# Sharing the 64-row remainder of two products in one step of the array

## The chip, the cores and the metric

The kernel runs on one core of a Trainium2 chip. The metric is the device time of one execution in microseconds (us); the kernel before took 552.86 us, the median of three runs (552.03 to 553.38). The change counts as seen where it moves this time by more than the runs differ.

## The reference

The input `x` has 2048 rows of 448 features. The output is `g * a + (1 - g) * b`, with a gate `g` per row, an attention with a compressive memory (`a`) and a feed-forward network (`b`). Cut to what matters:

```python
q, k, v = x @ wq, x @ wk, x @ wv       # 448 -> 448 = 16 heads of 28
for s in range(4):                     # segments of 512 rows
    p = softmax(qs @ ks.T * scale + mask)
    a_mem = (phi(qs) @ M) / (phi(qs) @ z + 1e-6)
    o = sigmoid(beta) * a_mem + (1 - sigmoid(beta)) * (p @ vs)
    M, z = M + phi(ks).T @ vs, z + phi(ks).sum()
a = o @ wo                             # 448 -> 448
b = silu(x @ w1) @ w2                  # 448 -> 1792 -> 448
g = sigmoid((x * gate_w).sum(-1))
```

Everything is float32. Five products have the 448 features as the dimension that is summed over: q, k, v (with the gate's weights as an extra column), the first half of the feed-forward network, and the output projection `o @ wo`.

## The kernel before

**Products.** Each float32 operand is scaled by a power of two and split into two float16 halves, a high one and a low one (what the rounding left over). A product is then the sum of high x high, low x high and high x low. The 448 features are three chunks of 128 rows and a remainder of 64. For a chunk of 128 the three terms are three matmuls. The remainder is stored twice, in partitions 0 to 63 and again in 64 to 127. Of `x` the remainder's slot has the high half above and the low half below (`x16`, L526), and the weights' two slots have their high half twice and their low half twice. So two matmuls of 128 rows do the remainder: the one with the weights' high half gives high x high and high x low, the other gives low x high (and low x low). A product is 3 x 3 + 2 = 11 matmuls (`passes`, L369; `product`, L532, whose matmuls all have L540).

**Which products there are.** `proj` (L798) makes q and k of one group of four heads and one segment: 128 output rows, 512 columns, 16 products each, in the `mm` banks of PSUM. The 16 rows of a group that q and k leave free carry the last 128 columns of the network's first weights. `vproj` (L852) makes v of 128 rows of `x`: 450 columns, 16 products, in the `sc` banks. `unit` (L1051) makes a block of 128 of the network's 1792 inner features for one segment, 512 columns, in the `mm` banks; after these products it adds up the second half of the network (L1086). `last_part` (L1280) projects the attention's output of 128 rows with `wo`, 448 columns, in the `sc` banks. `halves` (L513) makes the high and low halves of an operand: one instruction on ScalarE for the high half, one on VectorE, or two on GpSimd, for the low half. `features` (L554) does so for the attention's output and has it transposed by a DMA.

**Stages.** `project` loads `x` and the weights, finds their largest values (`scales`, L399, which spreads a value over all partitions with a matmul of one or two rows at L427), makes q, k, v and the memory, and stores them in DRAM. The second stage runs the attention of 16 groups and, between its matmuls, the first pass of the feed-forward network: 10 of the 14 blocks, in four segments. Then the second pass takes the three blocks left (and the one that came with q and k) and adds everything up.

**Order.** A planner (`Sched`) writes the instructions of each engine in a fixed order. It simulates the five queues from costs in the code: a task becomes ready when what it depends on has ended, and of the ready tasks the one with the lowest priority number goes first. A product is four tasks: one for each chunk of three matmuls, one for the remainder's two. Rings of buffers (`Ring`, `Buf`) hold a task back until a buffer is free; PSUM has three `mm`, three `sc` and two `cc` banks at first (L38) and four, three and one later (L39). The numbers at the head of the file (VF, VS, OT1 and so on) shift priorities; they change nothing in what is computed.

Of the kernel before, what the change touches and what calls it, by code (L numbers as in the profile page):

```python
# [46 lines left out]
WOT = -23.27  # L47
# [9 lines left out]
LOP = 33.77  # L57
LATE = 0.08
FIRST = 104.18
WPRIO = 134.65  # L60
MAXO = 62.72
# [3 lines left out]
MP = 34.45  # L65
# [11 lines left out]
XH0 = -8.84  # L77
XLD = -11.75
# [6 lines left out]
PRICE = 25.59  # L85
PVRUNS = [((1, 0), 1)]
PVP = 81.22
FLO = -69.24
FHI = 869.75
WOP = 155.66  # L90
SZ = 30.78
# [3 lines left out]
XLEAD = 146.82  # L95


class Ring:
    def __init__(self, n, make, shared=True):
        self.n, self.make, self.seq, self.shared = n, make, [], shared  # L100
# [7 lines left out]
class Task:  # L108
    def __init__(self, eng, dur, fn, deps, takes, uses, prio, lat, port):
        self.costs = {eng: dur} if isinstance(eng, str) else dict(zip(eng, dur))  # L110
        self.eng, self.fn, self.prio, self.lat, self.port = None, fn, prio, lat, port
        self.deps, self.takes, self.bufs = deps, takes, set(takes) | set(uses)
        self.banks = [b for b in self.bufs if not b.ring.shared]
        self.end, self.nd, self.succ = None, 0, []
        self.lead, self.tail = 0.0, 1.0


class Sched:
# [36 lines left out]
    def start_of(self, t, eng):  # L155
        s = max(self.ready(t, eng), self.free[eng])
        for b in t.takes:
            q = b.ring.seq
            k = len(q) - b.ring.n
# [34 lines left out]
    def run(self, until=None):  # L194
        wait = set(until) if until is not None else None
        while wait is None or wait:
# [29 lines left out]
            for b in t.takes:  # L226
                b.ring.seq.append(b)
                b.v = b.ring.make()
# [18 lines left out]
def infini_mix(ctx: ExitStack, tc: tile.TileContext, x, wq, wk, wv, wo, beta, w1, w2, out):  # L247
# [119 lines left out]
    X16 = {s: base.tile([128, 7, L], F16, name=f"xh{s}") for s in range(NSEG)}  # L367
# [158 lines left out]
    def x16(s, c, prio):  # L526
        ALL, END = slice(None), slice(REM, 128)
        r, d = XR.pop((s, c))
        lo = [((ALL, 4 + c), (ALL,), (ALL, c)) if c < NC else ((END, NC), (END,), (END, NC))]
        XH[s, c] = halves(NSEG - 1 - s, (ALL, c), lo, lambda: X16[s], lambda: r.v, L, d, prio, uses=[r])  # L530

    def product(ps, pairs, cols, prio, deps=(), takes=(), uses=(), cuts=None, kind=None):  # L532
        kind = kind or ful
        cuts = cuts or [3] * (NC) + [2]
        last, i0, n = None, 0, sum(cuts)
        for c, m in enumerate(cuts):
            def go(i0=i0, m=m):
                p = pairs()
                for i in range(i0, i0 + m):
                    nc.tensor.matmul(ps(), *p[i], start=(i == 0), stop=(i == n - 1))  # L540
            d = deps[c] if isinstance(deps, dict) else deps
            last = pe(kind(cols, m), go, last, *d, takes=takes if c == 0 else (), uses=tuple(takes) + tuple(uses), prio=prio)
            i0 += m
        return last

# [8 lines left out]
    def features(ol, half2, ot, ready, prio):  # L554

        sc, edge = os[:, 1:2], NC * 128
        hi = copy(D + 110, lambda: nc.scalar.activation(half2.v[:, :D], ol.v, AF.Copy, scale=sc), *ready, takes=[half2],
                  uses=[ol], prio=prio)

        def lo(e):  # L560
            rest(e, half2.v[:, D:L], ol.v[:, edge:], sc, half2.v[:, edge:D])
# [12 lines left out]
    def get_wa(f, ring, prio, *deps, got=None):  # L574
        (r, d), w = got or fetch_wa(f, prio, *deps), Buf(ring)

        def v():
            return r.v.rearrange("p (a b) -> p a b", a=4)
        WA[f] = (w, halves(W1, (slice(None), slice(0, 4)), [((slice(None), slice(4, 8)), (slice(None),), (slice(None), slice(0, 4)))],
                           lambda: w.v, v, L, d, prio, takes=[w], uses=[r]))  # L580
        return WA[f][1]
# [93 lines left out]
    def project():  # L675
# [88 lines left out]
        def whalves(name, prio, places):  # L764
            ALL = slice(None)
            for c, (b, _, v) in enumerate(places):
                k = dict(prio=prio + 0.01 * c)
                if name == "v":
                    def dst():
                        return W["v"][:, :, :D]  # L770
                    WS[name][c] = halves(WV, (ALL, c), [((ALL, 4 + c), (ALL,), (ALL, c))], dst, lambda v=v: v()[:, :D], D,
                                         SCALED[WV], uses=[b], **k)
                    continue
# [4 lines left out]
                for j, sl, n in ((WQ if name == "q" else WK, slice(0, GW), D), (HQ if name == "q" else HK, slice(GW, 128), 64)):  # L778
                    def src(v=v, sl=sl):
                        return v().rearrange("p (g e) -> p g e", g=NG)[:, :, sl]  # L780
                    WS[name][c] += halves(j, (ALL, c, ALL, sl), [((ALL, 4 + c, ALL, sl), (ALL,), (ALL, c, ALL, sl))], dst, src, n,
                                          SCALED[j], uses=[b], **k)
# [13 lines left out]
        PQ, PK, VB, MH, RT = {}, {}, {}, {}, {}  # L796

        def proj(t, which, prio):  # L798
            s, g = divmod(t, NG)
            w = W[which][:, :, g * 128:(g + 1) * 128]  # L800
            ps, hl = Buf(BK["mm"]), Buf(R["stg"])
            need = (s > 0) if which == "q" else (s < NSEG - 1)
            p = product(lambda: ps.v, lambda: passes(w, X16[s]), L, prio,
                        deps={c: WS[which][c] + XH[s, c] for c in range(NC + 1)}, takes=[ps], kind=half)
# [47 lines left out]
        def vproj(k, prio):  # L852
            s, tb = divmod(k, TB)
            ps, v = Buf(BK["sc"]), Buf(VT)
            p = product(lambda: ps.v[:, :D + 2],
                        lambda: passes(W["v"], X16[s][:, :, tb * 128:(tb + 1) * 128], True), D, prio,
                        deps={c: WS["v"][c] + WS["g"] + XH[s, c] for c in range(NC + 1)}, takes=[ps], kind=half)
# [120 lines left out]
        for t in range(NT):  # L978
# [5 lines left out]
            proj(t, "q", o)  # L984
            proj(t, "k", o + 1)
            if g == 0:
                for k in range(TB):
                    vproj(s * TB + k, VP(o, k))
# [55 lines left out]
    WAR2 = tiles(fp, "wa2", [128, 8, 128], F16, len(PASSES[0]) - NA)  # L1044
# [6 lines left out]
    def unit(s, fs, prio, finish, gate=(), tail=False):  # L1051
        gt = {}
        t1, t2 = {}, {}
        for f in fs:
            if f == FREE:
                gt[f] = spare(s, prio(0), m)
                continue
            p0 = prio(11 * L)
            ps, th, g = Buf(BK["mm"]), Buf(TH), Buf(GTR)
            w, wd = WA[f]  # L1060
            m = product(lambda ps=ps: ps.v, lambda w=w: passes(w.v, X16[s]), L, p0, deps=wd + PREV,
                        takes=[ps, g], uses=[w], kind=half)
# [10 lines left out]
            PREV[:] = [m]  # L1073
# [206 lines left out]
    def last_part(s, tb, ps, lasts, prio):  # L1280
        k = s * TB + tb
        ol, pl, oh, ot, pw, a, y = Buf(OL), Buf(PL), Buf(OH), Buf(OT), Buf(BK["sc"]), Buf(AR), Buf(YR)
        pr = prio - WOP
        rows = slice(tb * 128, (tb + 1) * 128)
        more = (Buf(ML), attended, amscr[s][:, tb]) if s else None
        d1 = load_o(ol, oscr[s][rows, :], *OST[s], PRE.get("o"), more=more, prio=pr - WOP)
        d2 = dma(229e3, lambda: start(pl.v, pscr[s][rows, :]), PST[k], *attended, PRE.get("p"),
                 takes=[pl], prio=pr - WOP)
        PRE.update(o=d1, p=d2)
        ft = features(ol, oh, ot, [d1, outer, PRE.get("f")], pr - WOT)  # L1290
        m = product(lambda: pw.v[:, :D], lambda: passes(wos.v, ot.v, True), D, pr,
                    deps={c: ft + WOS[c] for c in range(NC + 1)}, takes=[pw], uses=[ot], kind=half)
# [78 lines left out]
```

## Time and profile before

| what | before |
|---|---|
| median of three runs | 552.86 us (552.03 to 553.38) |
| profiled execution | 551.7 us from the first to the last instruction; the profile gives no other time of it |
| TensorE matmuls | 4009, busy 534.8 us (97%) |
| VectorE, ScalarE, GpSimd | busy 409.3, 391.8 and 354.7 us |
| mean granted TensorE clock | 0.984 of full speed |

PE is TensorE and PEld its weight loads, DVE is VectorE, ACT ScalarE, POOL GpSimd and SP SyncE, which issues the DMAs. A matmul's own duration reaches to its modelled end, and neighbours overlap; what a matmul costs in a dense stream is the distance from its start to the next one's. A row of the order of time gives the start in us, the length in us, the engine, the line, the operation, what is written from what, the array's rows and columns in use, the moving operand, and how many like it follow each other.

### The profile page before, as it was taken

What the parts mean: (1) busy time and instruction counts of PE and PEld (TensorE: products, weight loads), DVE (VectorE), ACT (ScalarE), POOL (GpSimd) and SP (SyncE); (2) the same over time, 40 slices, a digit from 0 to 9 for tenths busy, and PEclk for the clock granted to TensorE, in tenths of its full rate; (3) what the DMA queues carried; (4) which work ended last, traced back from release to release, by engine and by line L of the source; (5) the groups of instructions that cost most, each with busy time, mean ns of one, the idle gap of its engine ahead of it and who ended that gap; (6) DMA issues with size and microseconds to landing.
All of it is one profiled execution on the core that took longest, in us unless ns stands there. A gap on an engine that the chain in (4) does not pass through costs nothing.

```text
span 551.7 us, 11563 instructions
## 1 busy us (share of the span) xinstructions
PE 534.8 (97%) x4009; PEld 294.7 (53%) x4009; DVE 409.3 (74%) x1074; ACT 391.8 (71%) x688; POOL 354.7 (64%) x519
## 2 busy tenths in 40 slices
PE   4699999999999999999999999999999999999997
PEld 1234655655554556555665555655555555555444
DVE  6889999899789966777666779766987319646473
ACT  1588898986656977899877997878998896402140
POOL 2063254845830689988999987999999995213120
PEclk8689999999999999999999999999999999999999
DMA  8658998885586434312433234434301515698962
GB/s 276 205 175 227 203 236 233 225 226 166 170 233 162 146 100 137 87 42 80 121 102 102 58 98 124 121 103 112 100 18 53 138 49 152 219 241 212 225 160 83
DMA packets 89194, 81.68 MB, mean 148 GB/s; under 512 B 55176, under 2 KB 78856, under 8 KB 89136
## 3 DMA queue, kind: packets, MB, share of 16 engines
q1 hardware_dynamic: 89136, 80.95, 53.1%
q8 instruction: 31, 0.51, 0.4%
q14 instruction: 27, 0.22, 0.1%
HBM read 48.41 MB, written 26.09 MB: 135 GB/s over the span
## 4 chain that ended last, share of the span: by engine, by line
PE 89%; DVE 4%; DMA 4%; ACT 1%; issue 1%; SPq 0%; DVEq 0%; ACTq 0%
PE mm L540 31%; PE mm L1086 23%; PE sc L540 12%; PE sc L1182 6%; PE sc L644 6%; PE cc L1216 6%; DMA rawf<-in_w_dram 2%; PE cc L932 1%; DMA xraw<-in_x_dram 1%; PE cc L895 1%; DVE sizes L388 1%; DVE sc L654 1%; DMA v_scr<-vt 1%; PE sc L640 1%; PE cc L933 0%
## 5 line engine op out<-in xcount | busy, mean ns | idle before, releaser
L1203 POOL TENSOR_TENSOR phl<-pf,phl 128x384 f16<-128x384 f32 (+1 forms) x192 | 189.5, 1008 | 16.2 <-ACT phl L1199 16.2
L1086 PE MATMUL mm<-wb,ghl 128*128 128x448 f16 (+1 forms) x684 | 148.8, 349 | 0.0
L540 PE MATMUL mm<-xh,wa 128*128 128x512 f16 x572 | 141.4, 379 | 0.0
L1187 ACT ACTIVATE pf<-sc,es 128x512 f32<-128x512 f32 (+1 forms) x192 | 109.7, 623 | 19.8 <-PE sc L1182 18.6
L654 DVE CUSTOM_DVE_ANT_0 sc<-sc,mk 128x384 f32<-128x384 f32 (+1 forms) x192 | 104.8, 572 | 20.4 <-PE sc L644 19.1
L1086 PEld LDWEIGHTS <-ghl 128*128 128x128 f16 x684 | 65.0, 97 | 52.5 <-DVE ghl L508 0.3
L1199 ACT ACTIVATE phl<-pf 128x1280 f16<-128x1280 f32 x64 | 81.3, 1277 | 14.9 <-POOL pf L1193 14.9
L540 PEld LDWEIGHTS <-wa 128*128 128x128 f16 x572 | 53.6, 97 | 54.4 <-issue 1.4
L1182 PE MATMUL sc<-ring 86*128 86x512 f16 (+3 forms) x256 | 59.3, 299 | 0.4 <-ACT pf L1187 0.2
L644 PE MATMUL sc<-ring 84*128 84x128 f16 (+3 forms) x256 | 58.2, 299 | 0.1
L1224 DVE TENSOR_REDUCE oraw<-cc 128x116 f32<-128x232 f32 x64 | 25.3, 395 | 30.8 <-PE cc L1216 30.6
L1063 ACT ACTIVATE th<-mm,ths 128x512 f32<-128x512 f32 x52 | 35.8, 699 | 16.0 <-PE mm L540 15.8
L1216 PEld LDWEIGHTS <-phl 128*128 128x128 f16 x1280 | 41.9, 96 | 9.1
L540 PE MATMUL mm<-xh,wqs 128*128 128x512 f16 x176 | 44.5, 390 | 1.0 <-ACT wqs L516 0.7
L551 POOL TENSOR_TENSOR ol<-ol,ml 128x448 f32<-128x448 f32 x12 | 13.7, 1138 | 48.7 <-DMA ol<-o_scr 37.2
L1065 DVE SCALAR_TENSOR_TENSOR mm<-th,mm 128x512 f32<-128x512 f32 x52 | 35.7, 694 | 10.9 <-ACT th L1063 10.9
L1216 PE MATMUL cc<-vg,phl 128*128 128x29 f16 (+1 forms) x1280 | 43.6, 182 | 0.0
L540 PE MATMUL sc<-wvs,xh 128*128 128x450 f16 x176 | 39.9, 368 | 3.1 <-ACT wvs L516 2.1
L540 PE MATMUL mm<-xh,wks 128*128 128x512 f16 x176 | 42.1, 380 | 0.0
L1069 DVE SCALAR_TENSOR_TENSOR ghl<-mm,ghl 128x512 f16<-128x512 f32 x52 | 35.1, 683 | 5.6 <-ACT ghl L1067 5.2
L1182 PEld LDWEIGHTS <-ring 86*128 86x128 f16 x256 | 23.8, 97 | 22.0 <-issue 1.1
L1067 ACT ACTIVATE ghl<-mm 128x512 f16<-128x512 f32 x52 | 30.9, 604 | 6.5 <-DVE mm L1065 6.4
(165 smaller groups left out, 835.9 us busy)
## 6 DMA issues: line engine op xcount, KB each, us to landing
rawf<-in_w_dram SPq DMA_DIRECT2D x26, 256.0 KB
rawf<-in_w_dram SPq DMA_DIRECT2D x28, 224.0 KB
xraw<-in_x_dram SPq DMA_DIRECT2D x16, 256.0 KB
v_scr<-vt SPq DMA_DIRECT2D x16, 232.0 KB
vg<-v_scr SPq DMA_DIRECT2D x16, 232.0 KB
q_scr<-stg SPq DMA_DIRECT2D x16, 224.0 KB
ring<-q_scr SPq DMA_DIRECT2D x16, 224.0 KB
k_scr<-stg SPq DMA_DIRECT2D x16, 224.0 KB
```

What stands on the lines that cost most here:

```text
L540: nc.tensor.matmul(ps(), *p[i], start=(i == 0), stop=(i == n - 1))
L644: nc.tensor.matmul(ps.v[:, u:u + n], rg.v[:KS, 0, hh, i * 128:(i + 1) * 128], rg.v[:KS, 1, hh, :n], start=(i > 0), stop=(i > 0 or j == 3), ...
L654: nc.vector.tensor_tensor_reduce(r, r, MK[:, L - n:], 1.0, NEG, OP.add, OP.max, mx.v[:, hh, i:i + 1])
L1063: e1 = sact(L, lambda ps=ps, th=th: nc.scalar.activation(th.v, ps.v, AF.Tanh, scale=ths[:, s:s + 1]), m, DER[s], takes=[th], uses=[ps], pr ...
L1065: e2 = dve(L, lambda ps=ps, th=th: nc.vector.scalar_tensor_tensor(ps.v, th.v, 1.0, ps.v, op0=OP.add, op1=OP.mult), e1, uses=[ps, th], prio=p0)
L1069: e4 = dve(L, lambda ps=ps, g=g: nc.vector.scalar_tensor_tensor(g.v[:, 1], ps.v, DOWN, g.v[:, 0], op0=OP.mult, op1=OP.subtract), e3, uses= ...
L1086: nc.tensor.matmul(ps.v[:, lo:hi], g.v[:, y, sl], w.v[:, z, lo:hi], start=(j == 0 and i == 0), stop=(j == len(fs) - 1 and i == 2))
L1182: nc.tensor.matmul(ps.v[:, e:e + w], rg.v[:KK, 1, hh, j * 128:(j + 1) * 128], rg.v[:KK, 0, hh, j * 128:], start=True, stop=True)
L1187: ex.append(sact(e, lambda b=b, ps=ps, pf=pf, e=e: nc.scalar.activation(pf.v[:, b, :e], ps.v[:, :e], AF.Exp, scale=es[:, s:s + 1]), m, *ex ...
L1199: hi = copy(1280, lambda hl=hl, flat=flat: nc.scalar.activation(hl.v[:, 0], flat(), AF.Copy), *mk, takes=[hl], uses=[pf], prio=p0 + 2)
L1203: low = pool(w - u, lambda hl=hl, flat=flat, u=u, w=w: nc.gpsimd.tensor_sub(hl.v[:, 1, u:w], flat()[:, u:w], hl.v[:, 0, u:w]), low, uses=[ ...
L1216: nc.tensor.matmul(p[:, i, :2 - z], hl.v[:, z, u:u + 128], vg.v[:, j, hh, :2 - z], start=(z == zs[0] and i == 0), stop=(z == zs[-1] and j ...
```

## The change

The remainder's terms are dealt out anew. The weights' slot now has the high half in one half of its rows and the low half in the other, and `x` has its high half in both halves of one slot and its low half in both halves of another. One matmul of 128 rows gives high x high and low x high; high x low is left for a matmul of 64 rows. Low x low falls away. Two products (a and b) form a pair: a's ten full matmuls, then one joint step with a's 64-row matmul in partitions 0 to 63 and b's in 64 to 127, each into its own PSUM bank, then b's ten full matmuls. Pairs are two groups of q, two of k, two row blocks of v, two blocks of the network, and two row blocks of the output projection. With three blocks in the second pass one block per segment has no partner; its 64-row matmul stands alone (`product2` with `b` as `None`).

The planner counts the joint step as one matmul. A pair of one kind begins after the joint step of the pair before it, and while a pair is open, its ring keeps a bank for b. The weights' preparation follows the new layout: the low half of the last chunk is made for 64 rows only, in some places as an instruction of its own; v gets one copy (`same`), and every other block of the output projection gets a second instruction on ScalarE. `x` takes eight slots for seven, and one tile for weights seven for eight. The priority numbers are drawn anew, and the memory reserved for another kind of DMA descriptors is set to 4096 bytes.

```diff
-WOT = -23.27
+SCRATCH = 4096
+QB = 2.0
+KA = 1.93
+KB = 4.0
+WOT = 40.43
...
-FIRST = 104.18
-WPRIO = 134.65
-MAXO = 62.72
+FIRST = 96.7
+WPRIO = 137.54
+MAXO = 75.89
...
-VF = 0.02
-VA = 1.68
-VS = 15.54
+VF = 0.61
+VA = 0.01
+VS = 20.73
 NV = 8
-XS0 = 16.16
-VC = -4.07
-OT1 = -16.51
-XS = 17.15
-QS = -15.23
+XS0 = 13.14
+VC = -72.55
+OT1 = 4.96
+XS = 15.92
+QS = -18.08
...
-WOP = 155.66
+WOP = 27.88
...
+            if b.ring.open is not None and b is not t.closes and k >= b.ring.open - 1:
+                return None
...
-    def passes(w, a, flip=False):
+    X16 = {s: base.tile([128, 8, L], F16, name=f"xh{s}") for s in range(NSEG)}
+
+    HALF = (slice(0, REM), slice(REM, 128))
+
+    def passes(w, a, last=(NC, NC)):
+
         r = []
         for c in range(NC):
             r.append((w[:, c], a[:, c]))
             r.append((w[:, 4 + c], a[:, c]))
             r.append((w[:, c], a[:, 4 + c]))
-        r.append((w[:, NC], a[:, NC]))
-        r.append((w[:, 4 + NC], a[:, NC]))
-        return [(z, y) for y, z in r] if flip else r
+        r.append((w[:, last[0]], a[:, last[1]]))
+        return r
...
+    def chunks(x, before, first, pair=False):
+
+        last = None
+        for c, m in enumerate([3] * NC + [1]):
+            def go(c=c, m=m):
+                p = x.pairs()
+                for i in range(3 * c, 3 * c + m):
+                    nc.tensor.matmul(x.view(), *p[i], start=(first and i == 0), stop=(not first and i == 3 * NC),
+                                     skip_group_check=True)
+            last = pe(half(x.cols, m), go, last, *(before if c == 0 else ()), *x.deps[c],
+                      takes=x.takes if first and c == 0 else (), uses=x.uses, prio=x.prio)
+            if pair and c == 0:
+                last.opens = x.takes[0]
         return last
+
+    def product2(a, b=None, before=()):
+
+        last = chunks(a, before, True, b is not None)
+
+        def go():
+            z, y = a.rest(0)
+            nc.tensor.matmul(a.view(), z, y, start=False, stop=True, skip_group_check=True)
+            if b:
+                z, y = b.rest(1)
+                nc.tensor.matmul(b.view(), z, y, start=True, stop=False, skip_group_check=True)
+        joint = pe(half(a.cols), go, last, *(b.deps[NC] if b else ()), takes=b.takes if b else (),
+                   uses=a.uses + (b.uses if b else []), prio=a.prio)
+        joint.closes = b and b.takes[0]
+        return joint, (chunks(b, (joint,), False) if b else None)
...
+            rest(e, half2.v[:, el], ol.v[:, edge:], sc, half2.v[:, eh])
...
+        ALL, E = slice(None), HALF[1 - f % 2]
+        lo = [((ALL, slice(4, 4 + NC)), (ALL, slice(0, NC)), (ALL, slice(0, NC))), ((E, NC), (E, NC), (E, NC))]
...
+                def same(e):
+                    e.tensor_copy(W["v"][HALF[0], 4 + NC], W["v"][HALF[0], NC])
+                WS["v"][NC] = WS["v"][NC] + [either(D // 2, same, *WS["v"][NC], *WS["g"], prio=prio + 0.1)]
...
+            if g % 2 == 0:
+                proj(t, "q", (o, o + QB))
+                proj(t, "k", (o + KA, o + KB))
```

More of the change, by code (lines that the diff above doesn't have):

```diff
@@ L226, in run @@
             for b in t.takes:
+                if b is t.opens or b is t.closes:
+                    b.ring.open = len(b.ring.seq) if b is t.opens else None
                 b.ring.seq.append(b)
@@ L526, in x16 @@
     def x16(s, c, prio):
-        ALL, END = slice(None), slice(REM, 128)
+        ALL = slice(None)
         r, d = XR.pop((s, c))
[L529 to L543, printed above, removed]
-        return last
+        XH[s, c] = halves(NSEG - 1 - s, (ALL, c), [((ALL, 4 + c), (ALL,), (ALL, c))], lambda: X16[s], lambda: r.v, L, d, prio,
+                          uses=[r])
@@ L1053, in unit @@
         t1, t2 = {}, {}
[L1054 to L1062, printed above, removed]
+        blocks = [f for f in fs if f != FREE]
+        ends = {}
+        for f in blocks[::2]:
+            two, gs = [], [Buf(GTR) for _ in blocks[f - blocks[0]:][:2]]
+            for i, g in enumerate(gs, f):
+                p0, ps = prio(11 * L), Buf(BK["mm"])
+                w, wd = WA[i]
+                gt[i] = g
+                two.append(Prod(ps, lambda ps=ps: ps.v, lambda w=w: passes(w.v, X16[s]),
+                                lambda h, w=w: (w.v[HALF[h], NC], X16[s][HALF[h], 4 + NC]), L, p0, wd, takes=[] if two else gs, uses=[g, w]))
+            done = product2(*two, before=PREV)
+            PREV[:] = done[:1]
+            for x, end in zip(two, done):
+                ends[f + two.index(x)] = x.takes[0], x.prio, end
+        for f in blocks:
+            ps, p0, m = ends[f]
+            th, g = Buf(TH), gt[f]
             e1 = sact(L, lambda ps=ps, th=th: nc.scalar.activation(th.v, ps.v, AF.Tanh, scale=ths[:, s:s + 1]), m, DER[s], takes=[th],
```

144 lines of the change are left out of this document (96 added, 48 removed).

## The prediction

> **What bounds the kernel now.** I read the page first, then busy time by stage, then the matmuls by form, then the order of single matmuls where the array changes its use. On the page:
>
> ```profile
> span 551.7 us, 11563 instructions
> PE 534.8 (97%) x4009; PEld 294.7 (53%) x4009; DVE 409.3 (74%) x1074; ACT 391.8 (71%) x688; POOL 354.7 (64%) x519
> ...
> PE 89%; DVE 4%; DMA 4%; ACT 1%; issue 1%; SPq 0%; DVEq 0%; ACTq 0%
> ```
>
> TensorE is busy 97% of the span and carries 89% of the chain that ended last. The sum is made against this execution, whose only time is its span of 551.7 us; the median of the runs, 552.86 us, stands 1.2 us above it, and I add the change to the median. By stage (columns: stretch and its length, busy us of each engine with its instructions, granted clock, DMA share, GB/s):
>
> ```profile
> 0.00:33.00 33.00, 20.26 (x68) 7.69 (x69) 25.66 (x77) 14.18 (x33) 8.09 (x33) 0.74 0.70 237
> 33.00:190.00 157.00, 156.84 (x880) 85.30 (x879) 142.78 (x356) 123.61 (x258) 77.00 (x124) 1.00 0.76 203
> 190.00:440.00 250.00, 249.71 (x2393) 145.14 (x2392) 180.19 (x537) 210.90 (x329) 231.77 (x322) 1.00 0.34 93
> 440.00:551.70 111.70, 108.02 (x672) 56.53 (x670) 60.68 (x107) 43.10 (x69) 37.80 (x43) 1.00 0.61 168
> ```
>
> ```profile
> 548.06 0.81 DVE L1297 SCALAR_TENSOR_TENSOR y<-mm,ogs,ya 128x224 f32<-128x224 f32 x2 [0.47 <-PE mm L1086]
> ```
>
> From 33 us on TensorE misses 0.16, 0.29 and 3.68 us, the last nearly all behind its last matmul, which this DVE row at 548.06 waits for and the output's transfer follows. What it gains there the kernel gains, and what it loses the kernel loses. The other engines have room: the nearest, POOL, has 18 us left in the third stage. Only the first 33 us wait for others. But busy time overlaps between neighbours, so the price of a matmul has to be read from starts (start us, length, then the group and its count):
>
> ```profile
> 519.71 1.68 PE L540 MATMUL sc<-wos,oT 128*128 128x448 f16 x8
> 521.22 2.97 PE L540 MATMUL mm<-xh,wa 128*128 128x512 f16 x13
> ```
>
> Eight matmuls of 448 columns take the 1.51 us to the next start, 0.189 each. Thirteen of 512 take 2.97 with the last one's full length of 0.38, so (2.97 - 0.38)/12 = 0.216 each.
>
> **What is removed.** The products over the 448 features:
>
> ```profile
> L540 PE MATMUL mm<-xh,wa 128*128 128x512 f16 x572 | 141.4, 379 | 0.0
> L540 PE MATMUL mm<-xh,wqs 128*128 128x512 f16 x176 | 44.5, 390 | 1.0 <-ACT wqs L516 0.7 <-DVE wqs L508 0.3
> L540 PE MATMUL mm<-xh,wks 128*128 128x512 f16 x176 | 42.1, 380 | 0.0
> L540 PE MATMUL sc<-wvs,xh 128*128 128x450 f16 x176 | 39.9, 368 | 3.1 <-ACT wvs L516 2.1 <-DVE wvs L508 0.9
> L540 PE MATMUL sc<-wos,oT 128*128 128x448 f16 x176 | 35.4, 353 | 0.0
> ```
>
> A product is 11 matmuls, so these are 52 FFN products (13 blocks, 4 segments) and 16 each for q, k, v and o. A pair goes from 22 full matmuls to 20 and one joint step. The FFN gives 5 pairs per segment in the first pass (10 blocks), and one pair and one single in the second (3 blocks): 24 pairs and 4 singles. With 8 pairs each for q, k, v and o there are 40 pairs of 512 columns and 16 of 448 or 450. Were a joint step as cheap as one full matmul, 40 x 0.216 + 16 x 0.189 = 11.7 us would go.
>
> **What a joint step costs.** No step of 64 rows is in the trace. Its neighbours lie on both sides. Above are steps of 86 rows, below the steps of one or two rows in the scaling (L427):
>
> ```profile
> 127.86 1.46 PE L540 MATMUL mm<-xh,wqs 128*128 128x512 f16 x6
> 129.25 0.17 PE L427 MATMUL cc<-diag,oneb 2*128 2x2 bf16 x1
> 129.35 1.25 PE L540 MATMUL mm<-xh,wqs 128*128 128x512 f16 x5
> 130.44 0.81 PE L540 MATMUL mm<-xh,wks 128*128 128x512 f16 x3
> ```
>
> ```profile
> 342.81 0.73 PE L1086 MATMUL mm<-wb,ghl 128*128 128x448 f16 x3
> 343.47 0.17 PE L427 MATMUL cc<-diag,oneb 1*128 1x1 bf16 x1
> 343.57 0.74 PE L1086 MATMUL mm<-wb,ghl 128*128 128x448 f16 x3
> 344.15 0.27 PE L1182 MATMUL sc<-ring 86*128 86x256 f16 x1
> 344.26 0.73 PE L1086 MATMUL mm<-wb,ghl 128*128 128x448 f16 x3
> ```
>
> From 127.86 to 130.44 lie 11 full matmuls and one L427: 2.58 - 11 x 0.216 = 0.206 us for L427, which streams two columns. In the second place 1.34 - 6 x 0.189 = 0.206 us again. The 86-row step behind it takes 0.11 us for 256 columns, with nothing added. The weight loads tell why (start, length):
>
> ```profile
> 343.46 0.09 PEld L427 LDWEIGHTS <-oneb 1*128 1x128 bf16 x1 [0.37 <-issue]
> 343.57 0.10 PEld L1086 LDWEIGHTS <-ghl 128*128 128x128 f16 x1
> ...
> 343.57 0.11 PEld L1086 LDWEIGHTS <-ghl 128*128 128x128 f16 x2
> ```
>
> L427's load has nothing to wait for, yet it starts at 343.46, 0.08 us after the last full matmul has streamed (342.81 + 3 x 0.189 = 343.38), and the next full load waits until 0.10 us after L427's matmul. So the array empties before and after, where full loads otherwise run under the matmul ahead. I take 0.206 us as the price of going into row tiles and out again. The bounds are that of 86 rows (nothing) and this one; I take this one, since 86 rows cannot share the array in halves and a step that uses a part of the rows as a tile is what both L427 and the joint step are. Of the two 64-row matmuls the second can follow by the distance of two loads that do not wait for each other: the last row has two loads of 0.10 us in 0.11, so 0.015 us. The bounds for that are 0 and a whole load, 0.10.
>
> "Changing tiling mode (not just tile) drains the TensorE" is how the Trainium skill has it in TensorEngine Tiling (Array Packing), Key Properties. By that rule the 64-row step pays like L427 and the sum is the one below; by the 86-row rows it would be 541.5 us, which is the first rival. The skill's TensorE: Matmul & The Clock Gate, Part 3, gives about 4 ns between tiles; no run here shows it, and with it the sum would be 0.6 us lower.
>
> A joint step of 512 columns then costs 0.206 + 0.216 + 0.015 = 0.437 us where two full matmuls took 0.432; one of 448, 0.410 against 0.378. A single keeps 11 steps, the last of them a 64-row one: 0.206 more. Sum: 40 x 0.005 + 16 x 0.032 + 4 x 0.206 = 0.20 + 0.51 + 0.82 = **+1.5 us**. The gain of 11.7 us is paid back in changes of the array's use.
>
> **What is added beside it.** Nearest rows:
>
> ```profile
> L508 DVE SCALAR_TENSOR_TENSOR wa<-rawf,up,wa 128x512 f16<-128x512 f32 x12 | 10.9, 917 | 1.9 <-ACT wa L516 1.9
> L508 DVE SCALAR_TENSOR_TENSOR oh<-ol,os,oh 128x64 f16<-128x64 f32 x15 | 4.5, 303 | 4.9 <-ACT oh L557 4.9
> L557 ACT ACTIVATE oh<-ol,os 128x448 f16<-128x448 f32 x16 | 10.7, 669 | 34.3 <-POOL ol L551 34.3
> ```
>
> The low half of each FFN weight block becomes two instructions: 13 x 0.30 = 4 us on DVE or POOL, as do those of the q and k weights' last chunk (at most 4 x 0.3). Eight odd blocks of o get a second ACT instruction, at most 8 x 0.67 = 5.4 us. DVE is idle for 70 us of the third stage and ACT for 69 of the last, so these cost nothing; uncovered, each delays its product by its own length. One copy of the v weights (448 columns, at most the 0.92 us of a wa block) stands ahead of the first v product's last chunk; nine earlier matmuls of 0.19 or more cover it. No DMA is added or moved to another queue, and evictions keep their number. A pair takes its second bank at the joint step, some 0.2 us before b's first full matmul; what waits behind a missing bank is all of TensorE, but with four mm banks in the FFN (L39) and no wait of the FFN products in the groups above, I cost it at nothing.
>
> **The redrawn order** can only count in the head, and it is there that the rows show room:
>
> ```profile
> 23.93 2.26 PE L540 MATMUL sc<-wvs,xh 128*128 128x450 f16 x11
> ...
> 27.21 0.27 PE L418 MATMUL cc<-ident,most 128*2 128x128 f32 x1 [0.43 <-DVE most L414]
> 28.21 0.39 PE L540 MATMUL mm<-xh,wqs 128*128 128x512 f16 x1 [0.73 <-ACT wqs L516]
> 28.89 2.21 PE L540 MATMUL mm<-xh,wqs 128*128 128x512 f16 x5 [0.29 <-DVE wqs L508]
> 31.03 0.18 PE L427 MATMUL cc<-diag,oneb 2*128 2x2 bf16 x1
> 31.15 1.45 PE L540 MATMUL mm<-xh,wqs 128*128 128x512 f16 x3
> 32.40 1.34 PE L540 MATMUL sc<-wvs,xh 128*128 128x450 f16 x6
> ```
>
> TensorE idles 0.43 + 0.73 + 0.29 = 1.45 us, and after that matmuls of 512 columns come every 0.43 us (28.89 to 31.03, five), twice their price, for nine of them until 32.40: 9 x 0.21 = 1.9 us. A v product more as filler would save up to 3.4 us; one less (11 x 0.19) would cost 2.1. The scale of v's gate is moved up (VC), which frees v's banks earlier, the others of segment 0 move back (OT1); I take -0.5 us. Forecast: 552.86 + 1.5 - 0.5 = **553.9 us**, no measurable change.
>
> **The rivals.** *The array does not empty for 64-row tiles.* For it: steps of 86 rows cost nothing extra. Against: L427. Then -11.7 + 56 x 0.015 - 0.5 = -11.4, 541.5 us; were only one of the two passages free, 60 x 0.103 = 6.2 less than forecast, 547.7. *The second tile's load waits.* The second matmul starts a whole load after the first, 0.10 for 0.015, at 56 places: +4.8, 558.7 us, slower. It is decisive from 0.03 us of distance on (553.9 + 56 x 0.015 = 554.7). For it: L427's load too started only when it was alone. Against: the two overlapping loads at 343.57. *The tiles run one after the other*, which would mean that the change does not do what it says: 40 x 0.201 + 16 x 0.174 = 10.8 more, 564.7. Nothing in the trace excludes it. *The head is filled*: all 3.4 us gone, 2.9 below the forecast, 551.0; the v matmuls that already stand in it speak for it, v's three banks against.
>
> **How the numbers follow.** Chances: forecast 0.48 (its own range 552 to 556), no emptying 0.14, one passage free 0.08, head filled 0.08, load waits 0.16, one after the other 0.06. About 0.3%, 1.7 us, is what a measurement of this kernel can tell: the bounds are 551.2 and 554.5. Faster: 0.14 + 0.08 + 0.05 of the filled head + 0.03 of the forecast = 0.30. Slower: 0.16 + 0.06 + 0.14 of the forecast = 0.36. The rest, 0.34, is no change. The range leaves out no emptying and one after the other (0.20) and reaches past one free passage and the waiting load, with an us or less of the head on either side: 547 to 559.5.
>
> **What would show it.** In the trace after: x520 where x572 stood, 160 in place of each 176, and 64-row matmuls at the joint line, 116 in all; their first load some 0.1 us after the stream before it has ended, the two starts some 0.015 us apart, the next full load 0.1 us after the stream's end, and 0.44 us from joint step to next start. Loads that run under the matmul ahead would show the first rival, starts 0.1 apart the second, 0.2 apart the third. TensorE should stay without idle time from 33 us on; stalls for a bank would make the forecast wrong in a way that I have not priced.

## The result and the profile after

| | before | after |
|---|---|---|
| median of four runs each | 552.57 us (552.03 to 553.38) | 557.75 us (557.30 to 559.27) |
| ratio, 95% interval | | 1.0095 [1.0077, 1.0113] |
| profiled execution, span | 551.7 us | 557.6 us (the other three: 555.6 to 556.4) |

The change makes the kernel slower by 0.95%, 5.2 us by the medians and 5.9 us between the two profiled executions, each of them the longest of its four. The forecast was 553.9 us, counted from 552.86 us, the median of three of the four runs before. First the page of the kernel after:

```profile
PE 535.5 (96%) x4009; PEld 284.6 (51%) x4009; DVE 416.0 (75%) x1090; ACT 394.2 (71%) x696; POOL 349.6 (63%) x519
...
PE 81%; DVE 10%; POOL 2%; DMA 2%; ACT 2%; issue 1%; SPq 0%; DVEq 0%; POOLq 0%
```

TensorE is busy 0.7 us longer with the same number of matmuls, and VectorE's part of the chain that ended last has gone from 4% to 10%. Hardly any work became longer; waits came. Where, the stages tell. The kernel after, by stretch (length, busy us of PE, PEld, DVE, ACT and POOL with their instructions, granted clock, DMA share, GB/s):

```profile
0.00:33.00 33.00, 21.36 (x80) 8.01 (x80) 26.37 (x81) 13.73 (x32) 8.04 (x35) 0.79 0.68 220
33.00:140.00 107.00, 105.81 (x608) 55.55 (x606) 96.51 (x252) 88.97 (x198) 55.39 (x92) 1.00 0.81 213
140.00:160.00 20.00, 18.00 (x103) 9.58 (x103) 18.82 (x47) 10.45 (x22) 10.57 (x17) 1.00 0.66 195
...
180.00:200.00 20.00, 17.64 (x130) 9.08 (x129) 19.85 (x56) 13.96 (x22) 10.43 (x14) 1.00 0.48 137
200.00:440.00 240.00, 238.93 (x2269) 136.34 (x2267) 175.20 (x515) 203.19 (x320) 216.80 (x305) 1.00 0.34 94
440.00:557.60 117.60, 113.75 (x732) 57.08 (x730) 62.64 (x108) 48.16 (x81) 42.62 (x50) 1.00 0.57 161
```

The kernel before, in those of the same stretches that the prediction does not show:

```profile
33.00:140.00 107.00, 107.00 (x612) 59.27 (x611) 101.07 (x267) 88.56 (x195) 55.52 (x90) 1.00 0.81 210
140.00:160.00 20.00, 20.00 (x114) 11.45 (x113) 15.48 (x32) 11.45 (x22) 14.58 (x24) 1.00 0.65 194
...
180.00:200.00 20.00, 19.94 (x165) 11.29 (x164) 16.95 (x46) 17.46 (x29) 13.82 (x18) 1.00 0.50 144
200.00:440.00 240.00, 239.71 (x2286) 139.06 (x2284) 172.13 (x513) 203.22 (x317) 224.03 (x313) 1.00 0.34 92
```

Length less busy time is what TensorE idles:

| us | before | after | difference |
|---|---|---|---|
| 0 to 33 | 12.74 | 11.64 | -1.1 |
| 33 to 140 | 0.00 | 1.19 | +1.2 |
| 140 to 160 | 0.00 | 2.00 | +2.0 |
| 180 to 200 | 0.06 | 2.36 | +2.3 |
| 200 to 440 | 0.29 | 1.07 | +0.8 |
| 440 to the end | 3.68 | 3.85 | +0.2 |

With 0.10 us less in the stretch left out, the idle time grows by 5.2 us; with the 0.7 of busy time that is the 5.9 us. Nearly all of it is waits from 33 to 440 us, where before there were almost none. They repeat: a second profile of the same kernel (taken beside the late pairs below) idles 1.19, 2.00, 2.21 and 1.17 us from 33 to 140, 140 to 160, 180 to 200 and 200 to 440. In both stretches that lose 2 us VectorE has become nearly full: 18.82 of 20 us for 15.48, and 19.85 for 16.95. That alone makes no wait: from 33 to 140 us it was busy 101.07 of 107 us before, and TensorE idled 0.00.

The joint step itself, in the order of time (start us, length, group, count):

```profile
44.13 0.39 PE L572 MATMUL mm<-xh,wqs 64*128 64x512 f16 x1
44.13 0.39 PE L575 MATMUL mm<-xh,wqs 64*128 64x512 f16 x1
...
159.26 4.49 PE L558 MATMUL mm<-xh,wa 128*128 128x512 f16 x20
163.68 0.39 PE L572 MATMUL mm<-xh,wa 64*128 64x512 f16 x1
163.68 0.39 PE L575 MATMUL mm<-xh,wa 64*128 64x512 f16 x1
164.00 4.49 PE L558 MATMUL mm<-xh,wa 128*128 128x512 f16 x20
```

and the weight loads of the first one:

```profile
44.13 0.09 PEld L572 LDWEIGHTS <-wqs 64*128 64x128 f16 x1 [0.42 <-issue]
44.13 0.09 PEld L575 LDWEIGHTS <-wqs 64*128 64x128 f16 x1
44.45 0.55 PEld L558 LDWEIGHTS <-wqs 128*128 128x128 f16 x4 [0.23 <-issue]
```

The two 64-row matmuls start in the same hundredth, and so do their loads: the tiles do run at once. So it is at 54 of the 56 joint steps; at the other two the second starts 0.05 and 0.13 us later. But the twenty full ones have streamed at 159.26 + 20 x 0.216 = 163.58 and the step starts at 163.68, 0.10 later; and the next full load (44.45) waits until 0.10 after the step has streamed (44.13 + 0.216 = 44.35). The array empties on both sides. Steps of 448 columns do the same (16 x 0.189 us after 483.70 is 486.72):

```profile
483.70 3.19 PE L558 MATMUL sc<-wos,oT 128*128 128x448 f16 x16
486.82 0.36 PE L572 MATMUL sc<-wos,oT 64*128 64x448 f16 x1
...
487.12 2.07 PE L558 MATMUL sc<-wos,oT 128*128 128x448 f16 x10
```

A pair of 512 columns repeats after 164.00 - 159.26 = 4.74 us, and 22 full matmuls took 22 x 0.216 = 4.75.

Then the waits. All 1.19 us between 33 and 140 stand at 36 to 39 us, where k's products wait for the halves of k's weights. The last of them, on TensorE and on VectorE:

```profile
39.08 0.38 PE L558 MATMUL mm<-xh,wks 128*128 128x512 f16 x1 [0.42 <-DVE wks L519]
```

```profile
38.48 0.93 DVE L519 SCALAR_TENSOR_TENSOR wks<-wa,up,wks 64x224 f16<-64x224 f32 x2
```

These two instructions of 64 rows stand where the kernel before has one of 128 rows; they take 0.93 us, one of 128x448 at 34 us takes 0.67. The longest wait is at 154 us. TensorE, and what GpSimd does meanwhile:

```profile
152.68 1.51 PE L558 MATMUL sc<-wvs,xh 128*128 128x450 f16 x7
155.72 0.38 PE L1006 MATMUL cc<-mhl,phq 112*128 112x232 f32 x1 [1.54 <-POOL mhl L989]
156.67 2.33 PE L558 MATMUL mm<-xh,wa 128*128 128x512 f16 x10
```

```profile
152.21 1.35 POOL L983 TENSOR_TENSOR md<-md,bds 112x116 f32<-112x116 f32 x1 [0.20 <-DVE md L980]
...
154.02 1.27 POOL L901 TENSOR_TENSOR phq<-ph,phq 112x512 fp32r<-112x512 f32 x1
155.24 0.43 POOL L989 TENSOR_TENSOR mhl<-macc,mhl 112x116 fp32r<-112x116 f32 x1
```

The matmul that reads the memory (L1006) is in line before the copy of the memory that it needs is made. That copy is the last link of a chain of small steps on three engines, which began 0.20 us late behind VectorE. In the middle of it GpSimd spends 1.27 us on L901, which ends at 155.29 and makes the other operand (`phq`) of the same matmul: both come late on one engine. From 180 to 200 us it is shorter waits, the largest of them by cause (us in total, times, longest):

```profile
PE sc L1266 <- DVE mx L697: 0.8, 2, 0.5
```

Then come 0.7 us for ScalarE (L1271) and 0.7 for VectorE (L1152). The first is an attention matmul whose `sc` bank is still read by the reductions that find the rows' maxima (L697).

### The profile page after: what moved, and what is told of

The parts are those of the page before. It is cut to its first block, busy times and chain, and to the rows that moved or that the text cites. A ratio compares the mean times of both kernels' runs of the same rounds, so it can differ in the third digit from the quotient of the medians.

```text
span 557.6 us, 11613 instructions
## 1 busy us (share of the span) xinstructions
PE 535.5 (96%) x4009; PEld 284.6 (51%) x4009; DVE 416.0 (75%) x1090; ACT 394.2 (71%) x696; POOL 349.6 (63%) x519
## 4 chain that ended last, share of the span: by engine, by line
PE 81%; DVE 10%; POOL 2%; DMA 2%; ACT 2%; issue 1%; SPq 0%; DVEq 0%; POOLq 0%
PE mm L558 27%; PE mm L1170 21%; PE sc L558 10%; PE sc L1266 6%; PE cc L1300 5%; PE sc L687 5%; PE mm L572 2%; DVE sc L697 2%; POOL phl L1287 1%; DVE sizes L399 1%; DMA xraw<-in_x_dram 1%; PE cc L1006 1%; DVE stg L870 1%; PE sc L572 1%; PE cc L969 1%
## 5 line engine op out<-in xcount | busy, mean ns | idle before, releaser
L1287 POOL TENSOR_TENSOR phl<-pf,phl 128x384 f16<-128x384 f32 (+1 forms) x192 | 187.2, 998 | 13.9 <-ACT phl L1283 13.7
L558 PE MATMUL mm<-xh,wa 128*128 128x512 f16 x520 | 133.0, 379 | 0.0
L1271 ACT ACTIVATE pf<-sc,es 128x512 f32<-128x512 f32 (+1 forms) x192 | 109.0, 618 | 19.1 <-PE sc L1266 15.4
L697 DVE CUSTOM_DVE_ANT_0 sc<-sc,mk 128x384 f32<-128x384 f32 (+1 forms) x192 | 104.9, 571 | 17.5 <-PE sc L687 15.7
L558 PEld LDWEIGHTS <-wa 128*128 128x128 f16 x520 | 47.8, 97 | 49.6 <-issue 4.5
L687 PE MATMUL sc<-ring 84*128 84x128 f16 (+3 forms) x256 | 56.9, 299 | 0.1
L558 PE MATMUL mm<-xh,wqs 128*128 128x512 f16 x160 | 40.5, 380 | 0.7 <-POOL wqs L522 0.7
L1152 DVE SCALAR_TENSOR_TENSOR ghl<-mm,ghl 128x512 f16<-128x512 f32 x52 | 35.4, 683 | 6.9 <-ACT ghl L1150 6.6
L558 PE MATMUL sc<-wvs,xh 128*128 128x450 f16 x160 | 37.5, 370 | 2.9 <-ACT wvs L527 2.1
L558 PE MATMUL mm<-xh,wks 128*128 128x512 f16 x160 | 39.2, 380 | 1.1 <-POOL wks L522 0.7
```

Source lines behind the costliest of these rows:

```text
L558: nc.tensor.matmul(x.view(), *p[i], start=(first and i == 0), stop=(not first and i == 3 * NC), skip_group_check=True)
L687: nc.tensor.matmul(ps.v[:, u:u + n], rg.v[:KS, 0, hh, i * 128:(i + 1) * 128], rg.v[:KS, 1, hh, :n], start=(i > 0), stop=(i > 0 or j == 3), ...
L697: nc.vector.tensor_tensor_reduce(r, r, MK[:, L - n:], 1.0, NEG, OP.add, OP.max, mx.v[:, hh, i:i + 1])
L1152: e4 = dve(L, lambda ps=ps, g=g: nc.vector.scalar_tensor_tensor(g.v[:, 1], ps.v, DOWN, g.v[:, 0], op0=OP.mult, op1=OP.subtract), e3, uses= ...
L1271: ex.append(sact(e, lambda b=b, ps=ps, pf=pf, e=e: nc.scalar.activation(pf.v[:, b, :e], ps.v[:, :e], AF.Exp, scale=es[:, s:s + 1]), m, *ex ...
L1287: low = pool(w - u, lambda hl=hl, flat=flat, u=u, w=w: nc.gpsimd.tensor_sub(hl.v[:, 1, u:w], flat()[:, u:w], hl.v[:, 0, u:w]), low, uses=[ ...
```

## The experiments

Two theories were to be told apart first. By A, the joint step saves nothing, because the two changes of the array's use cost what the matmul saved. Then come the waits, put to the pairs (P: two products in one unit and two banks held) or to the redrawn numbers (N). Ratios are against the kernel before, run on the same chip; the kernel after was run on two chips.

### The same order without row tiles

Both matmuls of the joint step use all 128 rows, so nothing is shared. Each then also adds low x low. (The line of q and k; those of v, the network and the output projection change likewise.)

```diff
-lambda h, w=w: (w[HALF[h], NC], x[HALF[h], 4 + NC])
+lambda h, w=w: (w[:, NC], x[:, 4 + NC])
```

> The changed kernel in its own order, but each matmul of the joint step uses all 128 rows (it then adds low x low too), so the array is never split. Theory A (going into row tiles and out costs about 0.21 us and eats what the shared step saves): a joint step goes from 0.43 to 0.43 us at 512 columns, the four singles lose 0.2 each: 556.5 to 558, no change against the changed kernel. Theory B (the shared step is cheap and the slower time is all from waits): 56 steps become 0.2 us longer each, 567 to 569.

Measured: 558.04 us, 1.0100 [1.0081, 1.0118]; the kernel after had 1.0095. Its pair, in the order of time:

```profile
158.80 4.48 PE L558 MATMUL mm<-xh,wa 128*128 128x512 f16 x20
163.12 0.38 PE L572 MATMUL mm<-xh,wa 128*128 128x512 f16 x1
...
163.55 4.48 PE L558 MATMUL mm<-xh,wa 128*128 128x512 f16 x20
```

163.55 - 158.80 = 4.75 us, without a gap, for 4.74 with the shared step. Sharing the array saves nothing here, and it also isn't what makes the kernel slower: the 1% is all there without it, and so are the waits (1.15, 2.13, 1.98 and 1.07 us in the four stretches named above).

### The step issued twice, and both on the same rows

Two kernels measure the step by itself. In the first the 64-row matmuls are issued a second time behind the first two (the remainder's term counts twice):

```diff
 z, y = a.rest(0)
+nc.tensor.matmul(a.view(), z, y, start=False, stop=False, ...)
+if b:
+    zb, yb = b.rest(1)
+    nc.tensor.matmul(b.view(), zb, yb, start=True, stop=False, ...)
 nc.tensor.matmul(a.view(), z, y, start=False, stop=True, ...)
 if b:
...
+    nc.tensor.matmul(b.view(), zb, yb, start=False, stop=False, ...)
```

> The changed kernel with the matmuls of each joint step issued a second time directly behind the first (high x low is then counted twice). Theory A (the price is that of going into row tiles and out, once per step): each repeat costs one stream, 44 x 0.216 + 16 x 0.19 = 12.5 us: 569 to 571. Against it (each pair of 64-row matmuls pays by itself): 60 x 0.42 = 25 us: 582 to 584.

Measured: 568.73 us, 1.0290 [1.0266, 1.0314], a little below the 569 to 571 expected. TensorE's busy time is 548.1 us for 535.5: the 12.6 us more are the 12.5 expected, and the time grew by less because TensorE idles 2.7 us less than in the kernel after.

```profile
44.41 0.39 PE L572 MATMUL mm<-xh,wqs 64*128 64x512 f16 x1
...
44.63 0.38 PE L576 MATMUL mm<-xh,wqs 64*128 64x512 f16 x1
...
44.95 1.47 PE L558 MATMUL mm<-xh,wqs 128*128 128x512 f16 x6
```

The second two follow 0.22 us after the first two, one stream of 512 columns, and the full ones 0.32 after them as in the kernel after. The 0.2 us is paid once for going into row tiles and out, also when two steps are done there. In the second kernel b's matmul uses the rows of a's (so b's remainder reads the other half of its slot, low x low for high x low):

```diff
-z, y = b.rest(1)
+z, y = b.rest(0)
```

> The changed kernel with b's 64-row matmul of the joint step on the same 64 rows as a's (b then gets low x low in place of high x low). If the two tiles of a step do run side by side, this takes that away: 40 x 0.216 + 16 x 0.19 = 11.7 us more, 569. If they did not, nothing changes: 557 to 558.

Measured: 568.52 us, 1.0286 [1.0260, 1.0312]; expected was 569.

```profile
45.35 0.39 PE L572 MATMUL mm<-xh,wqs 64*128 64x512 f16 x1
45.57 0.38 PE L575 MATMUL mm<-xh,wqs 64*128 64x512 f16 x1
```

On the same rows the second starts 0.22 us later. So the common start of the kernel after is real sharing, worth 9.1 to 10.6 us (1.0286 less 1.0122 and 1.0095), and the passage takes it all back.

### The numbers without the pairs, and the pairs without the numbers

The kernel after with all numbers of before (for the three that are new, values that keep the old distances: `QB = 10.0`, `KA = 1.0`, `KB = 11.0`):

```diff
-VC = -72.55
+VC = -4.07
...
-OT1 = 4.96
+OT1 = -16.51
```

> The changed kernel with every priority number of the kernel before; the pair's partners get the priorities that their products had. Theory N (the redrawn numbers make the new waits at 150 and 185 to 197 us): the waits go, 553 to 554.5. Theory P (the pairs make them: the joint order of two products, the bank kept for the partner): the waits stay or others come, 556 or more. Theory C (the planner counts the joint step 0.21 us too cheap): 556 or more, since it still does.

and the kernel before with all numbers of after:

```diff
-VC = -4.07
+VC = -72.55
...
-OT1 = -16.51
+OT1 = 4.96
```

> The kernel before with the redrawn priority numbers and nothing else. Theory N: the same waits without pairs, 555 to 558. Theories P and C: 552 to 553.5, nearly the kernel before.

Measured: 566.31 us, 1.0249 [1.0230, 1.0268], and 569.66 us, 1.0313 [1.0292, 1.0334]. Stretches of the pairs with the old numbers:

```profile
33.00:140.00 107.00, 98.16 (x539) 49.55 (x536) 91.42 (x242) 81.92 (x179) 41.84 (x70) 0.98 0.73 192
```

and of the kernel before with the new ones:

```profile
140.00:160.00 20.00, 16.03 (x87) 10.10 (x87) 17.06 (x35) 10.72 (x22) 13.69 (x23) 0.88 0.66 190
...
180.00:200.00 20.00, 15.12 (x100) 7.03 (x99) 19.02 (x54) 11.19 (x19) 6.91 (x9) 0.91 0.55 147
```

The second shows waits in the two stretches of the kernel after (4.0 and 4.9 us for 2.0 and 2.4) with no pair in it: their place belongs to the order that these numbers make. The first has its waits elsewhere, 8.8 us between 33 and 140. Some of the loss is the clock: the granted clock fell to half for 13.6 us of the second after 155 us, and for 3.4 us of the first at 39. The first lies where P had it (556 or more), the second is far above what either theory forecast (555 to 558, 552 to 553.5). Neither P nor N alone holds: both mixtures are worse than either kernel, so numbers drawn for one work do not fit the other.

### The numbers drawn again for the step's real cost

The planner counts the joint step as one matmul, 0.2 us too little. Here it gets its cost, and all numbers are drawn again:

```diff
-joint = pe(half(a.cols), go, ...
+joint = pe([(half(a.cols)[0][0] + 0.21, 0.027)], go, ...
```

> The changed kernel with its pairs and joint steps as they are, the planner's cost of a joint step raised by 0.21 us to what the trace shows, and the priority numbers drawn once more for that cost. Theory N (the waits at 150 and 185 to 197 us are of the order that the numbers make, not of the pairs): they go, TensorE idles under 2 us between 33 us and its end, 552.5 to 555, no faster than the kernel before since the joint steps save nothing. Theory P (pairs force such waits under any numbers): 557 or more.

Measured: 558.13 us, 1.0104 [1.0083, 1.0125]. That is what P had (557 or more) and not N (552.5 to 555): the loss is the same.

```profile
140.00:160.00 20.00, 17.62 (x106) 10.20 (x105) 16.82 (x40) 10.55 (x22) 11.66 (x21) 1.00 0.58 174
```

The waits of 180 to 200 us are gone (TensorE is busy all 20.00), those of 140 to 160 have grown to 2.4 us. All in all TensorE idles 3.5 us from 33 to 440, in an execution of 556.85 us, the fastest of the four. Giving the step its price does not bring the time back; a second order with the same pairs loses about as much.

### Half the work of the maxima

The order of after, but VectorE's 192 reductions for the maxima (L697) read only the second half of their columns, so the softmax is shifted by another value. This takes away VectorE's load and no pair:

```diff
-r = ps.v[:, j * n:(j + 1) * n]
+r = ps.v[:, j * n + n // 2:(j + 1) * n]
```

> The changed kernel in its own order, but each of VectorE's 192 reductions of the scores' row maxima reads only the last half of its columns (the maxima over the other half are left out). Theory D (the waits at 185 to 197 us are VectorE, which is busy 99% there): about 0.2 us less for each of the 19 reductions in that stretch, 4 us in all, so the waits there fall from 3.7 to under 1 us, and the time by 2 to 3 us; the wait of 1.5 us at 154 for GpSimd's chain stays. Against it (a DMA or a bank): the waits at 185 to 197 us stay, and so does the time.

Measured: 555.68 us, 1.0059 [1.0037, 1.0081], 2.0 to 3.5 us less than the kernel after (1.0095 and 1.0122). The group between 180 and 200 us (count, busy us and mean ns of one, idle before), first the kernel before:

```profile
L654 DVE CUSTOM_DVE_ANT_0 sc<-sc,mk 128x384 f32<-128x384 f32 (+2 forms) x14 | 7.9, 576 | 2.3 <-PE sc L644 2.2
```

then the kernel after:

```profile
L697 DVE CUSTOM_DVE_ANT_0 sc<-sc,mk 128x512 f32<-128x512 f32 (+2 forms) x19 | 10.8, 603 | 0.1
```

and this one:

```profile
L697 DVE CUSTOM_DVE_ANT_0 sc<-sc,mk 128x256 f32<-128x256 f32 (+2 forms) x20 | 7.1, 383 | 0.9 <-PE sc L687 0.6
```

Before, VectorE waited 2.2 us for TensorE there; after, it has 19 of them to do for 14 and 0.1 us of idle time: TensorE waits for VectorE, not the other way round. Here are the stretches with the shorter reductions:

```profile
140.00:160.00 20.00, 18.00 (x93) 9.16 (x91) 18.57 (x48) 9.32 (x19) 10.38 (x18) 0.91 0.65 198
...
180.00:200.00 20.00, 19.52 (x162) 10.62 (x161) 18.68 (x60) 15.23 (x25) 12.69 (x17) 1.00 0.58 169
200.00:440.00 240.00, 239.88 (x2265) 136.77 (x2262) 145.91 (x510) 203.89 (x321) 219.82 (x307) 1.00 0.34 94
```

TensorE's idle time falls from 2.36 to 0.48 us and behind 200 us from 1.07 to 0.12, 2.8 us together. (The expectation spoke of 3.7 us of waits from 185 to 197; the idle time of the stretch was 2.36.) The 2.00 us from 140 to 160 stay: that wait is the chain over GpSimd.

### Pairs only where a product stands late

Pairs only in the feed-forward network and the output projection; q, k and v go one by one with a remainder on all 128 rows, as do the network's singles. The joint step has its cost in the planner, and the numbers are drawn again. The kernel after was run beside it.

```diff
-proj(t, "q", (o, o + QB))
+proj(t, "q", (o,))
...
-a.rest(0)
+a.rest(0 if b else 2)      # HALF[2] = slice(0, 128)
```

> Pairs and joint steps for the feed-forward network and the output projection alone (32 pairs); q, k and v each by itself again, with the matmul for the remainder on all 128 rows, as the four singles too; the joint step costed as the trace shows it, and the numbers drawn again for this. Theory S (what cannot be hidden is the pairing of q, k and v, which hands the memory and the retrievals of the last segment over late): the wait at 140 to 160 us goes, TensorE stays without a gap from 90 us on, 552.5 to 554.5. Theory P (pairs of either stage leave waits): 556 or more. A gain over the kernel before would speak against the price of the joint step.

> The changed kernel once more, on the chip of the run above: 556 to 559, slower than the run above by 3 to 5 us under theory S.

Measured: 554.75 us, 1.0038 [1.0022, 1.0055], and for the kernel after 559.55 us, 1.0122 [1.0103, 1.0142]. A stretch of the first:

```profile
33.00:140.00 107.00, 104.29 (x593) 56.69 (x592) 98.14 (x257) 88.06 (x194) 63.38 (x95) 1.00 0.80 211
```

4.8 of the 6.9 us come back, against the expectation slightly too few: the waits from 140 to 160 us are down to 0.7 us, but 2.7 us stand between 33 and 140, 2.4 of them before 90. Of the 4.8, four singles without a passage make 0.8 (4 x 0.19, below). The numbers differ too. The order drawn anew with all pairs lost 1.04%, so that pairing q, k and v causes the difference is likely, but it is not shown by itself.

### The steps of one and two rows on all rows

The prediction's price for a passage came from L427. If it is right, the kernel before gains by leaving the passage out there: the nine matmuls get 128 rows, of which the rest are zero.

```diff
-diag = const.tile([n, n], ...)
+diag = diags[:n, a:b]
...
-nc.tensor.matmul(ps.v[:, 256:256 + n], oneb[:n], diag, ...)
+nc.tensor.matmul(ps.v[:, 256:256 + n], oneb, diags[:, a:b], ...)
```

> The kernel before, but the nine matmuls of the scaling that use one or two rows use all 128 (ones against a matrix that is zero below those rows), in the same order. Theory A: each step in the dense stretch falls from 0.206 to about 0.03 us, seven of them: 1.2 us faster, 551.3, with the load of the next full matmul no longer late. Against A (those steps are dear because they wait for a scale, not because of their rows): no change, 552.6.

Measured over 12 runs: 551.48 us, 0.9985 [0.9973, 0.9997], faster than both kernels by a little. Its place in the order of time:

```profile
340.51 0.73 PE L1086 MATMUL mm<-wb,ghl 128*128 128x448 f16 x3
341.08 0.17 PE L427 MATMUL cc<-diags,oneb 128*128 128x1 bf16 x1
341.11 0.73 PE L1086 MATMUL mm<-wb,ghl 128*128 128x448 f16 x3
```

340.51 + 3 x 0.189 = 341.08: the step starts as the stream ends and takes 0.03 us where it took 0.206. Of the 1.2 us expected 0.7 came, and the interval reaches from 0.2 to 1.5.

## Why the prediction was right in its range and wrong in its reason

**The range held by luck.** 557.75 us lies between 547 and 559.5, but the upper end stood there for a second tile that loads late (558.7), and that rival fell. The forecast itself, 553.9 us and no measurable change, did not come: the kernel is slower, by waits that no rival had.

**What bounds the kernel.** Right: TensorE, from 33 us on. But the sentence that what it loses the kernel loses was used for its own work alone. Nor is GpSimd, with 18 us left in the third stage, the engine with the least room: by the prediction's own row VectorE had 14.2 us left from 33 to 190 (157 less 142.78), and there most of the waits came.

**The joint step.** Right in kind, and nearly in size. Forecast were 0.437 us for the step and 4.757 for a pair; 0.42 (163.58 to 164.00) and 4.74 were measured. The emptying on both sides, the loads that wait for it and the common start of the tiles are in the rows; 28 + 24 matmuls of 64 rows in the network and 64 in the others make the 116. The first rival (no emptying), one free passage, the waiting load and the tiles one after the other fall with the same rows, and the kernel with both matmuls on the same rows shows what the last would have cost. A single's step takes 469.08 - 468.77 = 0.31 us from its start, and the 0.10 before it, so 0.19 more than a full matmul for 0.206:

```profile
468.77 0.39 PE L572 MATMUL mm<-xh,wa 64*128 64x512 f16 x1
469.08 2.33 PE L558 MATMUL mm<-xh,wa 128*128 128x512 f16 x10
```

A step of 448 columns takes 0.40 us (486.72 to 487.12) for 0.410. So by starts the sum is 40 x (0.42 - 0.432) + 16 x (0.40 - 0.378) + 4 x 0.19 = +0.6 us, where the prediction had +1.5. The 0.7 us of busy time do not measure it: the profiled execution before ran its head at half clock for 3.4 us (last section), which counts as busy. The Trainium skill's TensorEngine Tiling (Array Packing), Key Properties, says that a change of the tiling mode drains TensorE, and the trace agrees, with 0.10 us on each side. The Trainium skill's TensorE: Matmul & The Clock Gate, Part 3, has about 4 ns between tiles; the trace agrees, with less than 0.01 us at 54 of 56 steps, where the prediction took 0.015.

**The head.** Forecast -0.5 us; the idle time fell by 1.1, so the rival of a filled head (-3.4) fell too. But 1.9 of the 3.4 us were no room. The matmuls that came every 0.43 us ran while the granted clock was 0.50 (29.03 to 32.45), and the kernel before with the padded steps, which keeps the order, has a granted clock of 1.00 from 28 to 33 us.

**The step that failed** is "The redrawn order can only count in the head". The head was the only place where the rows of before showed room to gain, and from that I concluded that it was the only place where the order could change anything. A stage without idle time has nothing to gain from another order, but all to lose: from 33 to 440 us TensorE gave up 6.2 us (1.2 + 2.0 + 2.3 + 0.8 less 0.1). That is more than the 4.9 us by which the 5.9 of the profiled executions exceed the forecast's +1.0; the head and the busy time came out lower. The last sentence of the prediction named such stalls and left them without a price, for a missing bank alone.

**The added work costs nothing** failed with it. At 39 us TensorE waits 0.42 us for the two 64-row instructions on k's weights, of which up to 0.26 (0.93 less 0.67) are the added work, in a stretch without room; the prediction had said that uncovered work delays its product by its own length, and took it for covered. And I set the added instructions against DVE's 70 idle us in the third stage. From 180 to 200 us VectorE was busy 16.95 of 20 us before, and in the new order has 19.85. A mean over 250 us does not cover a stretch of 20. What filled it there is old work at another time, 10.8 us of maxima for 7.9, not the new instructions; the kernel with shorter maxima shows that VectorE's load from 180 us on is what TensorE waited for.

**What stays open.** The 1.5 us wait behind the chain over GpSimd is read from the trace, not taken away in a run. Two orders drawn for all pairs lose 1% each, and an order with fewer pairs 0.4%; whether the pairs leave no order without waits, or none was found, these runs can't tell. Why pairs and numbers together made the chain at 154 us late is open too.

## What to carry to other kernels

Two products that share a row-tiled step pay about 0.2 us for going in and out among full matmuls, as much as a 512-column matmul takes. A second joint step behind the same passage took 0.22 us for two matmuls, where two full ones take 0.43, so sharing should pay where several steps are done together; no kernel here was built for that. Steps of one or two rows were cheaper padded to 128: 0.03 us for 0.206. When the engine that sets the end has no idle time, a new order of its work must be priced as a risk over the whole span: ask for short stretches (20 us here), not for the whole stage, which other engine is nearly full and what small chain ends just in time. A list of priorities is a part of the kernel it was drawn for; to move it to other work, or other work under it, cost 2.5 to 3.1% here (a part of it by the clock), more than the change itself.

## What was not expected of the hardware

The matmul behind the 1.54 us wait is followed by ten of 512 columns, which take 2.33 us in the kernel after (156.67). In the kernel with the shorter maxima, after the same wait, the row is

```profile
156.21 4.01 PE L558 MATMUL mm<-xh,wa 128*128 128x512 f16 x10
```

and for 3.4 us the granted clock is half:

```profile
156.24:159.65 3.41, 3.41 (x11) 1.21 (x10) 2.49 (x10) 0.00 (x0) 1.36 (x4) 0.50 0.86 280
```

The head of the kernel before has such a stretch too, behind the waits of 0.43, 0.73 and 0.29 us that the prediction lists:

```profile
29.03:32.45 3.42, 3.42 (x10) 1.04 (x9) 3.32 (x8) 3.18 (x11) 3.16 (x6) 0.50 0.49 155
```

In both, TensorE idled about 1.5 us in the 3.4 us ahead of the stretch (1.54 at once, and 1.45 in three pieces). In the kernel after, the same 1.54 us brought no lower clock. So waits of this size can cost more than their length, 1.68 us more in the ten matmuls (4.01 for 2.33), in one execution and not in another. That the waits bring the clock down is read from the order of events and not tested by a run. The Trainium skill's TensorE: Matmul & The Clock Gate, Why this matters for your kernels, warns of idle gaps above about 3 us; these rows differ, with 1.54.

Few moving columns alone did not bring the passage, only few rows did: padded to 128 rows, L427 with one moving column takes 0.03 us.
